# Making one of VectorE's four shifted exp copies with an accumulating DMA instead of a GpSimd copy

## The chip, the cores and the metric

The kernel runs on one core of one Trainium2 chip. The metric is the device time of one execution in microseconds (us), as the median of several runs.

## The reference

A transformer block with conditioning: 2048 tokens, width 512, 32 heads of 16, a feed-forward width of 1792. Cut to what matters:

```python
h = layernorm(x) * (1 + ca) + sa                       # ca, sa, ... from silu(c) @ w_mod
q, k, v = split(h @ wqkv)                              # 32 heads of 16
p = softmax(einsum('bhqd,bhkd->bhqk', q, k) / 4)       # 32 x 2048 x 2048 exps
x = x + ga * ((p @ v) @ wo)
h = layernorm(x) * (1 + cb) + sb
x = x + gb * ((gelu(h @ w_gate) * (h @ w_up)) @ w_down)
```

The 134 million exps are the load. In tiles of 128 x 512 they are 2048 "blocks".

## The kernel before

The program is unrolled by a planner in Python. It keeps a model of when each engine is free and when each DMA lands, and records the instructions of every engine in the order that this model suggests. On the chip each engine then runs its list strictly in order and waits on semaphores, so a wait that the planner did not foresee holds up everything behind it on that engine. TensorE writes the scores to tiles in PSUM, the memory for its results; the room for one block of scores is called a bank here. Where TensorE would stand idle the planner may put "filler" matmuls, whose result nobody reads.

ScalarE makes most exps, two or three blocks in one instruction. VectorE makes some "quads" (four blocks, one per head of a group) in another way: it turns the score into the bit pattern of a bfloat16 power of two, with one multiply and add to uint16, and makes four more copies with a constant added to the pattern. The sum of the five stands for the exponential better than one does, and TensorE adds them up in its accumulation of P times V. The copies are these tasks:

```python
SHIFT = (20, 43, 69, 101)          # constants added to the bit pattern

def shift_task(self, q, i):
    def f():
        s = self.sq_free[0]
        self.ts(self.helper, self.sq[s].bitcast(U16), self.kq[q["k"]].bitcast(U16),
                1.0, float(SHIFT[i]), ALU.mult, ALU.add)        # 128 x 2048, uint16
        # ... slot s becomes ready for the value matmuls
    self.task([f], ("shift", q["rnd"][0]), lambda: bool(self.sq_free) and self.first(q))
```

In the kernel before, `pooled` gives a copy to GpSimd (`self.helper = "pool"`) when GpSimd is free and its 1900 ns would not collide with a VectorE instruction for a port that, in the model, the two engines share (`port_at`):

```python
            if self.port_at(max(x, self.free["pool"]), 1900, "pool") <= t + 100:
                f()
```

The model lets a DMA land a fixed time after the bytes of all earlier DMAs.

```python
        if op.stream not in COMPUTE:
            self.free[eng] = t + 460
            self.dma_free = max(t + 1400, self.dma_free) + cost / 350
            op.t1 = self.dma_free + LAND                       # LAND = 1500 ns
```

How the softmax denominators come back: when a unit (512 queries of 4 heads) ends, its row sums go to DRAM, come back spread over 128 partitions, are inverted on VectorE, go to DRAM again and come back broadcast over the partitions; then VectorE multiplies. These are four dependent DMA steps, all issued on SyncE's queue, and at their end VectorE, in order, waits for the last:

```python
        self.dma("sp", s1..., self.osb[DH:P:32, lo:hi], ...)      # scr_den <- osb
        # den <- scr_den;  rden = 1 / den (VectorE);  scr_rec <- rden
        # rb <- scr_rec, four DMAs of up to 64 KB, broadcast to 32 partitions each
        def fin2():
            self.tt("dve", self.onorm[:, qd, c:c + W], osb, rb, ALU.mult)
```

The softmax here doesn't subtract the row's maximum and nothing guards it: scores larger than these inputs give would overflow.

Of the kernel before, what the change touches and what calls it, by code (L numbers as in the profile page):

```python
# [6 lines left out]
ALU = mybir.AluOpType  # L7
BF16 = mybir.dt.bfloat16
# [5 lines left out]
P = 128  # L14
# [28 lines left out]
AHEAD = 24  # L43
PREFER = 300
LAND = 1500
WIDE = 0
PRESS = 6
HOT = 1
FLOOR = 3300
POOLED = 1  # L50
FIRST = 30
AHEAD1 = 12
LATE = 0
# [39 lines left out]
class _Recorder:  # L93


    def __init__(self, nc):
        self.nc = nc
        self.ops = []
        self.count = {}
        self.bystream = {}  # L100
        self.clock = {e: {} for e in ALLENG}
        self.hist = {}
        self.pitch = {}
        self.kind = {}
        self.sem = {}
        self.dry = False
        self.probing = None
        self.free = {e: 700.0 for e in ALLENG}
        self.dma_free = self.pe_issue = self.pe_end = 0.0
        self.pe_mode = None  # L110
        self.tile_free = [0.0] * 16
        self.log = []
        self.whole = False
        self.lock = False
        self.port = []
        self.locked = 0
        self.fetched = [0, 0.0]

# [155 lines left out]

    def model(self, op, t, cost):
        eng = op.eng
        if op.stream not in COMPUTE:
            self.free[eng] = t + 460
            self.dma_free = max(t + 1400, self.dma_free) + cost / 350
            op.t1 = self.dma_free + LAND  # L280
        elif eng == "pe":
            cols, rows, tp = cost
            mode = 0 if tp is None else (1 if rows == 32 else 2)
            t = max(t, self.pe_issue)
            if self.fetched[0] % 128 == 0 and t > 20000:
                t = self.fetched[1] = max(t, self.fetched[1] + 3750)
            self.fetched[0] += 1
            if mode != self.pe_mode:
                t = max(t, self.pe_end + 105)
            q = range(16)  # L290
            if mode == 1:
                q = range(tp[0] // 8, tp[0] // 8 + 4)
            elif mode == 2:
                q = range(tp[1] // 32, 16, 4)
            t = max(t, max(self.tile_free[i] for i in q))
            end = t + max(cols, 64) / 2.4
            for i in q:
                self.tile_free[i] = end
            self.pe_mode, self.pe_issue, self.pe_end = mode, t + (4 if mode else 27), max(self.pe_end, end)
            self.free[eng] = t  # L300
            self.log.append((t, cols if mode == 0 else cols / 4))
            op.t1 = end + 158
        else:
            self.free[eng] = t + cost
            op.t1 = t + cost + (107 if eng == "act" else 92)
# [104 lines left out]
    def dma(self, eng, out, in_, sem, noncontig=False):  # L410
# [7 lines left out]
            n *= int(k)  # L418
        return self.rec(eng, fn, [in_], [out], dma=sem, cost=n)

    def emit(self, final):
        for s in self.count:
            self.sem[s] = self.nc.alloc_semaphore(s)
# [33 lines left out]
class _Kernel(_Recorder):  # L457
# [12 lines left out]
    def alloc(self):  # L470
# [16 lines left out]
                     for b in range(2)] for x in range(2)]  # L487
        self.sq = [mreg[:, 4096 + 2048 * i:6144 + 2048 * i] for i in range(NS)]
        self.sq += [mreg[:, 2048 * i:2048 * i + 2048] for i in range(2)]
        self.wmod = [mreg[:, 0:NDC * 1024].rearrange("p (a n) -> p a n", a=NDC),  # L490
                     mreg[:, NDC * 1024:NDC * 3072].rearrange("p (a n) -> p a n", a=NDC)]
        dreg = sb("dreg", [P, NFC * D], BF16)
# [27 lines left out]
        self.tcol = sb("tcol", [P, NDC], FP32)  # L520
        self.asum = self.rden[:, 0:2, 0:6]
        self.sc_bf = sb("sc_bf", [P, NDC], BF16)
        self.scbc = sb("scbc", [P, NDC, P], BF16)[:, :, :]
        self.modA = sb("modA", [P, 8], FP32)
        self.modB = sb("modB", [P, 8], FP32)
        self.rm4 = self.den[:, 0, 0:4]
        self.rm = sb("rm", [P, 2], FP32)
        self.ident = sb("ident", [P, P], BF16)
        self.ones = sb("ones", [P, P], BF16)[:, :]
        self.self32 = sb("self32", [P, P], FP32)  # L530
        self.scp = ps("ps_sc", [P, SC, 512], FP32)
        self.pv = ps("ps_pv", [P, 512], FP32)
        self.mi = ps("ps_mi", [P, 512], FP32)
        self.scr1 = self.dram("scr_den", [4, 2048], FP32)
        self.scr2 = self.dram("scr_rec", [4, 2048], FP32)


    def prologue(self):
# [29 lines left out]
        self.ts(dve, self.rm[:, 0:1], self.rm[:, 1:2], -1.0, 1.0, ALU.mult, ALU.add)  # L568
        self.memset(pool, self.vaug[:, :, :].rearrange("p t (h c) -> p t h c", c=VW)[:, :, :, DH:VW], 1.0)

        for dc in range(NDC):
            self.mm(self.scp[:, 0, dc:dc + 1], self.crow[0:1, P * dc:P * dc + P], self.ones[0:1, 0:1])
        self.warm_up(16)
# [238 lines left out]
    def side_mod(self):  # L812
        mi = self.mi[:, :]
        if not self.dry:
            self.task([lambda dc=dc: self.ts("dve", self.scbc[:, dc, :], self.ones, self.sc_bf[:, dc:dc + 1],
                                             None, ALU.mult) for dc in range(NDC)], "scbc")
        yield from self.until("scbc")
        for dst, k, s in ((self.ga, 2, 1.0), (self.gb, 5, 0.5)):
            for dc in range(NDC):
                yield 512, lambda dc=dc, k=k: self.mm(mi, self.scbc[:, dc, :], self.mod_w(dc, 512 * k, 512),  # L820
                                                      start=(dc == 0), stop=(dc == NDC - 1))
            self.ts("dve", dst[:, :], mi, s, None, ALU.mult)
            yield END
        yield 512, lambda: self.mod_cols(mi[:, 0:8], 1536)
        self.copy("dve", self.modB[:, :], mi[:, 0:8])
        self.ts("dve", self.modB[:, 4:8], self.modB[:, 4:8], 1.0, None, ALU.add)
        self.done("modB")
        if not self.dry:
            self.sq_free.extend(range(NS))
        yield END  # L830

    def side_wo_load(self):
# [236 lines left out]
                n += next((i for i, s in enumerate(steps) if s[0] != "dve"), len(steps))  # L1069
        return n  # L1070

    def pooled(self, t):

        for tk in self.tasks:
            if tk[1] is None or tk[1][0] != "shift" or not tk[2]() or self.urgency(tk) == 0:
                continue
            f = tk[0][0][1]
            self.helper = "pool"
            x = self.probe(f)
            if self.port_at(max(x, self.free["pool"]), 1900, "pool") <= t + 100:  # L1080
                f()
                self.tasks.remove(tk)
                self.done(tk[1])
                self.helper = "dve"
                return
            self.helper = "dve"

    def background(self, t):
        if POOLED and self.free["pool"] < t and self.busy():
            self.pooled(t)  # L1090
        while self.step("sp", max(self.free["sp"], t) + 40):
            pass
        while self.free["dve"] <= t + 150 and self.step("dve", max(self.free["dve"], t) + 40):
            pass
# [79 lines left out]
    def stream(self):  # L1174
# [45 lines left out]
        wait = self.wait = []  # L1220
        self.quad_free = list(range(NK))
        self.sq_free = [NS, NS + 1]
        cand = [k for k, (u, r, g0) in enumerate(rounds) if u in units[:2] or QA <= r * (512 // u[3]) < QB]
        quad = None
        self.helper = "dve"
# [56 lines left out]
        def pv_do(x):  # L1282
# [10 lines left out]
            else:  # L1293
                q["ready"].remove((i, src))
                q["n"] -= 1
                if i and (q["slots"][i] < NS or "modB" not in self.have):
                    self.sq_free.append(q["slots"].pop(i))
                q["used"].discard(i)
                self.drop(q)
# [8 lines left out]
        while cg <= group[units[-1]]:  # L1308
# [16 lines left out]
            if tq is not None and tq <= t + 30:  # L1325
# [10 lines left out]
                if len(mem) == CH and pos >= FIRST and not self.pressed() and self.free["dve"] + 600 < max(self.free["act"], t + 480) + 880 + LATE:  # L1336
                    while quad is None and cand and rounds[cand[0]][2] < pos + (AHEAD1 if rounds[cand[0]][2] < nsplit else AHEAD):
                        cand.pop(0)
                    if quad is not None:
                        g = quad["rnd"][2]  # L1340
                    elif (cand and self.quad_free and (pos < ends[2] or self.credit < CREDIT) and rounds[cand[0]][2] < pos + 96 and self.backlog() < BACK
                          and all(k in self.have for k in self.keys(seq[rounds[cand[0]][2]]))):
                        rnd = rounds[cand.pop(0)]
                        quad = {"rnd": rnd, "j": list(range(4)), "k": self.quad_free.pop(0), "ready": [], "n": 5, "slots": {}, "used": set(range(5))}
# [2 lines left out]
                        g = rnd[2]  # L1347
                        vec.update(range(g, g + 4))
                        mem, after = take(CH)
                gb = s0 + CH - 1  # L1350
                if g is not None:
                    for n in (CH, CH - 1):
                        if n == CH and (s0 or not WIDE or pos < nsplit + 12
                                        or self.probe(lambda: self.mm(self.scp[:, SC - 1, 0:P], *filler)) > t + 30):
                            continue
                        mem, after = take(n)
                        js = [j for j in quad["j"] if j not in [seq[m][2] for m in mem]]
                        if js:
                            break
                    if n == CH:  # L1360
                        gb = SC - 1
                    j = (js or quad["j"])[0]
                    quad["j"].remove(j)
                    g += j
                items = [(m, s0 + i) for i, m in enumerate(mem)]
                if g is not None:
                    items.append((g, gb))
                self.require(sorted({k for m, _ in items for k in self.keys(seq[m])}))
# [8 lines left out]
                if g is not None:  # L1377
                    kq = self.kq[quad["k"]]
                    while (self.free["dve"] + 1260 <= self.free["act"] + SLIP
                           and self.step("dve", max(self.free["dve"], t) + 40)):  # L1380
                        pass
                    self.ts("dve", kq[:, 512 * j:512 * j + 512].bitcast(U16), self.scp[:, gb, :], 128 / OCT, SHIFT_C,
                            ALU.mult, ALU.add)
                    if not quad["j"]:
                        quad["ready"].append((0, [kq[:, 512 * x:512 * x + 512] for x in range(4)]))
# [48 lines left out]

    def qk(self, items):
        for kk in range(max(512 // it[0][0][3] for it in items)):
            for ((_, qd, q0, W), r, j), k in items:
                kpb = 512 // W
                if kk >= kpb:
                    continue  # L1440
                kt = r * kpb + kk
                dc, ee = qd // 2, qd % 2
                self.mm(self.scp[:, k, W * kk:W * kk + W],
                        self.km[ee][32 * j:32 * j + 32, dc, P * kt:P * kt + P],
                        self.qT[32 * j:32 * j + 32, dc, q0:q0 + W], tp=(32 * j, 0))

# [23 lines left out]
# [4 lines that stand above are left out]
            self.ts(self.helper, self.sq[s].bitcast(U16), self.kq[q["k"]].bitcast(U16), 1.0, float(SHIFT[i]), ALU.mult, ALU.add)  # L1474
            if self.probing is None:
# [3 lines left out]
                q["ready"].append((i + 1, [self.sq[s][:, 512 * x:512 * x + 512] for x in range(4)]))  # L1479
                self.drop(q)  # L1480
        self.task([f], ("shift", q["rnd"][0]), lambda: bool(self.sq_free) and self.first(q))

    def osb_span(self, u):

# [202 lines left out]
```

## Time and profile before

| | before |
|---|---|
| median of 3 runs | 843.27 us (843.14 to 844.77) |
| profiled span | 842.2 us |
| ScalarE busy | 810.1 us, 96% |
| TensorE busy | 780.4 us, 93% |
| VectorE busy | 710.2 us, 84% |
| shifted copies on VectorE, on GpSimd | 284, 60 |
| exp blocks on ScalarE, on VectorE | 1704, 344 (86 quads) |

The groups of the kernel before, shapes kept apart: count, busy time and mean ns of one, then the engine's idle time just before them.

```profile
L364 ACT ACTIVATE E<-ps_sc 128x1536 bf16<-128x1536 f32 x320 | 453.7, 1538 | 3.1 <-PE ps_sc L351 2.8
L364 ACT ACTIVATE E<-ps_sc 128x1024 bf16<-128x1024 f32 x372 | 366.0, 1133 | 1.5 <-PE ps_sc L351 1.4
...
L376 POOL TENSOR_SCALAR mreg<-dreg 128x2048 uint16<-128x2048 uint16 x43 | 81.5, 1898 | 309.3 <-DVE mreg L376 92.3 <-PE ps_sc L351 75.8 <-DVE wreg L376 67.1
```

Busy time over count, 453.7 / 320 = 1.418 us for three blocks and 366.0 / 372 = 0.984 us for two, is what the prediction below takes as the cost of one exp, so 0.434 us a block. Both are a little high. Neighbouring exps overlap, and where their shapes differ the overlap is counted in both groups: the two sum to 819.7 us, more than ScalarE's 810.1 us in all. From the end of one exp to the end of the next, where ScalarE did not idle between, the trace has medians of 1.343 and 0.917 us, so 0.426 us a block. The exps waited 4.6 us in all.

```profile
rb<-scr_rec SPq DMA_DIRECT2D x96, 64.0 KB, 2.0
...
scr_rec<-rden SPq DMA_DIRECT2D x24, 8.0 KB, 1.4
```

### The profile page before, as it was taken

What the parts mean: (1) busy time and instruction counts of PE and PEld (TensorE: products, weight loads), DVE (VectorE), ACT (ScalarE), POOL (GpSimd) and SP (SyncE); (2) the same over time, 40 slices, a digit from 0 to 9 for tenths busy, and PEclk for the clock granted to TensorE, in tenths of its full rate; (3) what the DMA queues carried; (4) which work ended last, traced back from release to release, by engine and by line L of the source; (5) the groups of instructions that cost most, each with busy time, mean ns of one, the idle gap of its engine ahead of it and who ended that gap; (6) DMA issues with size and microseconds to landing.
All of it is one profiled execution on the core that took longest, in us unless ns stands there. A gap on an engine that the chain in (4) does not pass through costs nothing.

```text
span 842.2 us, 28224 instructions
## 1 busy us (share of the span) xinstructions
PE 780.4 (93%) x12684; PEld 278.9 (33%) x12689; DVE 710.2 (84%) x1345; ACT 810.1 (96%) x747; POOL 117.7 (14%) x71
## 2 busy tenths in 40 slices
PE   8899999999999998989999999899998998988997
PEld 3333333322222222222222222222343333335556
DVE  7878899899899999999889999999887886376484
ACT  5999999999999999999999999999999999999982
POOL 1000102031220331142210130333000000000000
PEclk9999999999999999999999999999999999999999
DMA  9000000000003111111003111111013222185330
GB/s 315 13 27 17 16 15 15 17 15 15 15 16 90 44 36 52 52 41 46 16 28 96 52 53 32 48 40 40 27 25 103 78 72 65 37 235 158 92 96 14
DMA packets 74931, 47.68 MB, mean 57 GB/s; under 512 B 17693, under 2 KB 70618, under 8 KB 74810
## 3 DMA queue, kind: packets, MB, share of 16 engines
q1 hardware_dynamic: 72426, 44.30, 18.1%
q8 instruction: 99, 1.62, 0.8%
q10 hardware_dynamic: 2384, 1.57, 0.7%
q14 instruction: 22, 0.18, 0.1%
HBM read 43.25 MB, written 2.61 MB: 54 GB/s over the span
## 4 chain that ended last, share of the span: by engine, by line
ACT 79%; PE 12%; DVE 4%; DMA 3%; SPq 1%; issue 0%; DVEq 0%
ACT E L364 76%; PE ps_mi L351 5%; PE ps_sc L351 5%; ACT wreg L364 3%; PE ps_pv L351 2%; DMA rb<-scr_rec 1%; DMA scr_rec<-rden 1%; SPq L415 1%; DVE mreg L376 1%; DVE wreg L381 0%; DMA xs<-in_A_x_dram 0%; DMA mreg<-in_B_w_down_dram 0%; DVE st L404 0%; DVE wreg L368 0%; DVE dreg L376 0%
## 5 line engine op out<-in xcount | busy, mean ns | idle before, releaser
L364 ACT ACTIVATE E<-ps_sc 128x1024 bf16<-128x1024 f32 (+2 forms) x700 | 782.7, 1311 | 17.4 <-PE ps_sc L351 16.9
L351 PE MATMUL ps_sc<-qT,kmo 32*128 32x512 bf16 (+2 forms) x1408 | 171.9, 323 | 10.5 <-ACT E L364 9.3
L351 PE MATMUL ps_sc<-qT,kme 32*128 32x512 bf16 (+2 forms) x1344 | 162.1, 331 | 18.2 <-ACT E L364 16.5
L376 DVE TENSOR_SCALAR dreg<-ps_sc 128x512 uint16<-128x512 f32 x228 | 153.9, 685 | 21.3 <-PE ps_sc L351 19.6
L351 PE MATMUL ps_pv<-E,vaug 128*17 128x512 bf16 (+2 forms) x2308 | 157.1, 321 | 1.3 <-DVE vaug L385 0.8
L351 PE MATMUL ps_pv<-mreg,vaug 128*17 128x512 bf16 (+2 forms) x1644 | 129.1, 354 | 4.1 <-DVE mreg L376 3.1
L376 POOL TENSOR_SCALAR mreg<-dreg 128x2048 uint16<-128x2048 uint16 x43 | 81.5, 1898 | 309.3 <-DVE mreg L376 92.3
L351 PE MATMUL ps_mi<-wreg,mreg 128*32 128x512 bf16 (+1 forms) x1792 | 113.7, 355 | 10.2 <-DVE wreg L381 5.5
L376 DVE TENSOR_SCALAR mreg<-dreg 128x2048 uint16<-128x2048 uint16 x185 | 119.6, 683 | 3.1 <-PE ps_pv L351 2.8
L351 PEld LDWEIGHTS ps_sc<-qT,kme 32*128 32x128 bf16 x1344 | 42.8, 91 | 146.5 <-ACT E L364 123.0
L376 DVE TENSOR_SCALAR mreg<-ps_sc 128x512 uint16<-128x512 f32 x116 | 78.5, 685 | 14.9 <-PE ps_sc L351 13.8
L351 PEld LDWEIGHTS ps_sc<-qT,kmo 32*128 32x128 bf16 x1408 | 46.4, 91 | 128.0 <-ACT E L364 101.7
L351 PEld LDWEIGHTS ps_pv<-E,vaug 128*17 128x17 bf16 x2308 | 47.6, 89 | 62.9 <-issue 50.8
L376 DVE TENSOR_SCALAR mreg<-mreg 128x2048 uint16<-128x2048 uint16 x99 | 65.1, 686 | 3.0 <-PE ps_pv L351 2.5
L351 PEld LDWEIGHTS ps_mi<-wreg,mreg 128*32 128x32 bf16 x1792 | 39.4, 95 | 57.4 <-issue 18.9
L351 PEld LDWEIGHTS ps_pv<-mreg,vaug 128*17 128x17 bf16 x1644 | 37.5, 88 | 51.0 <-DVE mreg L376 24.5
L385 DVE CAST wreg<-ps_mi 128x512 bf16<-128x512 f32 x49 | 33.6, 687 | 15.9 <-PE ps_mi L351 15.6
L376 POOL TENSOR_SCALAR mreg<-mreg 128x2048 uint16<-128x2048 uint16 x17 | 32.3, 1897 | 93.8 <-DVE onorm L368 23.0
L381 DVE SCALAR_TENSOR_TENSOR wreg<-wreg,ps_mi 128x512 bf16<-128x512 bf16 x49 | 33.4, 682 | 12.8 <-PE ps_mi L351 5.6
L351 PE MATMUL ps_mi<-hreg,wreg 128*32 128x512 bf16 x480 | 39.5, 384 | 0.5 <-DVE qT L376 0.5
L351 PE MATMUL ps_mi<-wo,onorm 128*32 128x512 bf16 x480 | 36.6, 382 | 0.1
L368 DVE TENSOR_TENSOR wreg<-wreg 128x1024 bf16<-128x1024 bf16 (+1 forms) x56 | 34.1, 618 | 0.5
(138 smaller groups left out, 597.8 us busy)
## 6 DMA issues: line engine op xcount, KB each, us to landing
mreg<-in_B_w_up_dram SPq DMA_DIRECT2D x32, 256.0 KB, 3.1
mreg<-in_B_w_gate_dram SPq DMA_DIRECT2D x28, 256.0 KB, 2.9
rb<-scr_rec SPq DMA_DIRECT2D x96, 64.0 KB, 2.0
mreg<-in_B_w_down_dram SPq DMA_DIRECT2D x16, 256.0 KB, 2.8
dreg<-in_B_w_down_dram SPq DMA_DIRECT2D x12, 256.0 KB, 4.0
mreg<-in_w_mod_dram SPq DMA_DIRECT2D x1, 2048.0 KB, 14.4
out_dram<-xs SPq DMA_DIRECT2D x16, 128.0 KB, 1.8
rb<-scr_rec SPq DMA_DIRECT2D x52, 32.0 KB, 2.6
```

What stands on the lines that cost most here:

```text
L351: return self.rec("pe", lambda e: e.matmul(out, lhsT, rhs, start=start, stop=stop, tile_position=tp), [lhsT, rhs], [out], cost=(n, int(rhs ...
L364: return self.rec("act", lambda e: e.activation(out, in_, func, scale=scale, **kw), rd, wr, cost=self.cost("act", out, [in_], "act"))
L368: return self.rec(eng, lambda e: e.tensor_tensor(out, a, b, op), [a, b], [out], cost=self.cost(eng, out, [a, b], "tt"))
L376: return self.rec(eng, lambda e: e.tensor_scalar(out, a, s1, s2, **kw), rd, [out], cost=self.cost(eng, out, [a], "ts"))
L381: return self.rec("dve", lambda e: e.scalar_tensor_tensor(out, a, s, b, op0=op0, op1=op1), rd, [out], cost=self.cost("dve", out, [a, b], " ...
L385: return self.rec(eng, lambda e: e.tensor_copy(out, in_), [in_], [out], cost=self.cost(eng, out, [in_], "ts"))
L415: return e.dma_start(out, in_)
```

## The change

Its intent: free GpSimd, and with it the port that the model keeps apart. One copy of a quad is made by a DMA that *adds* the bit patterns to a slot that already holds the constant. A plain DMA on SyncE's queue presets the slot (512 KB, one row of DRAM broadcast to 128 partitions); an accumulating DMA on GpSimd's queue adds the quad. There are two such slots. A second, smaller part lets a VectorE block go to a spare PSUM bank, so that ScalarE keeps three blocks in that instruction. Cut to its core:

```diff
-POOLED = 1
+ADDS = (3, 2)            # which of the four constants, one slot each
+ADDGEN = 1200
+ADDTIME = 5000
+SIDE = 1024
@@ model
+        if op.stream not in COMPUTE and eng == "pool":
+            self.free[eng] = t + ADDGEN
+            self.add_free = op.t1 = max(t + 2000, self.add_free) + ADDTIME
@@
+    def dma_add(self, out, in_, sem):
+        return self.rec("pool", lambda e: e.dma_start(out, in_, accum_op=ALU.add), [in_, out], [out], dma=sem)
@@
+    def preset(self, a):
+        self.task([("sp", lambda: self.dma("sp", self.aq[a].bitcast(U16),
+                    self.steps[a:a + 1, :].broadcast_to([P, 2048]), "dp%d" % a))], ("preset", a))
+
+    def added(self, t):
+        for q in self.wait:
+            if self.plain[q["rnd"][0]] <= ADDLEFT or q["adds"] >= ADDMAX:
+                continue
+            for a in range(len(ADDS)):
+                i = ADDS[a]
+                if ("preset", a) not in self.have or q["tk"][i] not in self.tasks:
+                    continue
+                # ... takes the shift task away and lets the DMA do it
+                op = self.dma_add(self.aq[a].bitcast(U16), self.kq[q["k"]].bitcast(U16), "dk%d" % a)
+                return
@@ background
-        if POOLED and self.free["pool"] < t and self.busy():
-            self.pooled(t)
+        if self.free["pool"] < t:
+            self.added(t)
@@ the spare bank for VectorE's block
-                        if n == CH and (s0 or not WIDE or pos < nsplit + 12 ...):
+                        if n == CH and (self.open or self.credit > SIDE
+                                        or self.probe(lambda: self.mm(self.mi[:, 0:P], *filler)) > t + 30):
```

(The rest makes room for a 4 KB slot per partition and writes the constants to DRAM once.)

More of the change, by code (lines that the diff above doesn't have):

```diff
@@ L45 @@
 LAND = 1500
-WIDE = 0
+SIDE = 1024
 PRESS = 6
@@ L49 @@
 FLOOR = 3300
-POOLED = 1
+ADDS = (3, 2)
+ADDGEN = 1200
+ADDTIME = 5000
+ADDLEFT = 7
+ADDMAX = 1
 FIRST = 30
@@ L115, in __init__ @@
         self.port = []
+        self.add_free = 0.0
         self.locked = 0
@@ L276, in model @@
         eng = op.eng
-        if op.stream not in COMPUTE:
+        if op.stream not in COMPUTE and eng == "pool":
+            self.free[eng] = t + ADDGEN
+            self.add_free = op.t1 = max(t + 2000, self.add_free) + ADDTIME
+        elif op.stream not in COMPUTE:
             self.free[eng] = t + 460
@@ L489, in alloc @@
         self.sq += [mreg[:, 2048 * i:2048 * i + 2048] for i in range(2)]
+        self.aq = [sb("aq", [P, 2048], BF16)[:, :], self.sq[NS - 1]]
         self.wmod = [mreg[:, 0:NDC * 1024].rearrange("p (a n) -> p a n", a=NDC),
@@ L522, in alloc @@
         self.sc_bf = sb("sc_bf", [P, NDC], BF16)
-        self.scbc = sb("scbc", [P, NDC, P], BF16)[:, :, :]
+        self.scbc = dreg[:, 11 * D:12 * D].rearrange("p (a n) -> p a n", a=NDC)
         self.modA = sb("modA", [P, 8], FP32)
@@ L528, in alloc @@
         self.ident = sb("ident", [P, P], BF16)
-        self.ones = sb("ones", [P, P], BF16)[:, :]
+        self.ones = dreg[:, 10 * D:10 * D + P]
         self.self32 = sb("self32", [P, P], FP32)
@@ L535, in alloc @@
         self.scr2 = self.dram("scr_rec", [4, 2048], FP32)
+        self.steps = self.dram("scr_add", [len(ADDS), 2048], U16)
     def prologue(self):
@@ L569, in prologue @@
         self.memset(pool, self.vaug[:, :, :].rearrange("p t (h c) -> p t h c", c=VW)[:, :, :, DH:VW], 1.0)
+        for i, x in enumerate(ADDS):
+            self.memset(dve, self.rb[0:16, 64 * i:64 * i + 64].bitcast(U16), SHIFT[x])
+        for i in range(len(ADDS)):
+            self.dma(sp, self.steps[i:i + 1, :].rearrange("o (p n) -> (o p) n", p=16),
+                     self.rb[0:16, 64 * i:64 * i + 64].bitcast(U16), "add%d" % i)
         for dc in range(NDC):
@@ L828, in side_mod @@
         if not self.dry:
-            self.sq_free.extend(range(NS))
+            self.sq_free.extend(range(NS - 1))
+            if len(ADDS) > 1:
+                self.preset(1)
+            else:
+                self.sq_free.append(NS - 1)
         yield END
@@ L1070, in backlog @@
         return n
-    def pooled(self, t):
-        for tk in self.tasks:
-            if tk[1] is None or tk[1][0] != "shift" or not tk[2]() or self.urgency(tk) == 0:
-                continue
-            f = tk[0][0][1]
-            self.helper = "pool"
-            x = self.probe(f)
-            if self.port_at(max(x, self.free["pool"]), 1900, "pool") <= t + 100:
-                f()
-                self.tasks.remove(tk)
-                self.done(tk[1])
-                self.helper = "dve"
+    def preset(self, a):
+        self.task([("sp", lambda: self.dma("sp", self.aq[a].bitcast(U16), self.steps[a:a + 1, :].broadcast_to([P, 2048]), "dp%d" % a))],
+                  ("preset", a))
+    def added(self, t):
+        for q in self.wait:
+            if self.plain[q["rnd"][0]] <= ADDLEFT or q["adds"] >= ADDMAX:
+                continue
+            for a in range(len(ADDS)):
+                i = ADDS[a]
+                if ("preset", a) not in self.have or q["tk"][i] not in self.tasks:
+                    continue
+                self.have.discard(("preset", a))
+                self.tasks.remove(q["tk"][i])
+                op = self.dma_add(self.aq[a].bitcast(U16), self.kq[q["k"]].bitcast(U16), "dk%d" % a)
+                self.kq_at[q["k"]] = op.t1
+                q["slots"][i + 1] = -1 - a
+                q["adds"] += 1
+                q["done"] = q.get("done", 0) + 1
+                q["ready"].append((i + 1, [self.aq[a][:, 512 * x:512 * x + 512] for x in range(4)]))
+                self.drop(q)
                 return
-            self.helper = "dve"
     def background(self, t):
-        if POOLED and self.free["pool"] < t and self.busy():
-            self.pooled(t)
+        if self.free["pool"] < t:
+            self.added(t)
         while self.step("sp", max(self.free["sp"], t) + 40):
@@ L1222, in stream @@
         self.sq_free = [NS, NS + 1]
+        self.kq_at = [0.0] * NK
+        self.preset(0)
         cand = [k for k, (u, r, g0) in enumerate(rounds) if u in units[:2] or QA <= r * (512 // u[3]) < QB]
@@ L1295, in pv_do @@
                 q["n"] -= 1
-                if i and (q["slots"][i] < NS or "modB" not in self.have):
+                if i and q["slots"][i] < 0:
+                    self.preset(-1 - q["slots"].pop(i))
+                elif i and (q["slots"][i] < NS or "modB" not in self.have):
                     self.sq_free.append(q["slots"].pop(i))
@@ L1340, in stream @@
                         g = quad["rnd"][2]
-                    elif (cand and self.quad_free and (pos < ends[2] or self.credit < CREDIT) and rounds[cand[0]][2] < pos + 96 and self.backlog() < BACK
+                    elif (cand and self.quad_free and self.kq_at[self.quad_free[0]] <= t + 300 and (pos < ends[2] or self.credit < CREDIT) and rounds[cand[0]][2] < pos + 96 and self.backlog() < BACK
                           and all(k in self.have for k in self.keys(seq[rounds[cand[0]][2]]))):
@@ L1349, in stream @@
                         mem, after = take(CH)
-                gb = s0 + CH - 1
+                gb = self.scp[:, s0 + CH - 1, :]
                 if g is not None:
                     for n in (CH, CH - 1):
-                        if n == CH and (s0 or not WIDE or pos < nsplit + 12
-                                        or self.probe(lambda: self.mm(self.scp[:, SC - 1, 0:P], *filler)) > t + 30):
+                        if n == CH and (self.open or self.credit > SIDE
+                                        or self.probe(lambda: self.mm(self.mi[:, 0:P], *filler)) > t + 30):
                             continue
@@ L1360, in stream @@
                     if n == CH:
-                        gb = SC - 1
+                        gb = self.mi[:, :]
                     j = (js or quad["j"])[0]
@@ L1364, in stream @@
                     g += j
-                items = [(m, s0 + i) for i, m in enumerate(mem)]
+                items = [(m, self.scp[:, s0 + i, :]) for i, m in enumerate(mem)]
                 if g is not None:
@@ L1381, in stream @@
                         pass
-                    self.ts("dve", kq[:, 512 * j:512 * j + 512].bitcast(U16), self.scp[:, gb, :], 128 / OCT, SHIFT_C,
+                    self.ts("dve", kq[:, 512 * j:512 * j + 512].bitcast(U16), gb, 128 / OCT, SHIFT_C,
                             ALU.mult, ALU.add)
@@ L1436, in qk @@
         for kk in range(max(512 // it[0][0][3] for it in items)):
-            for ((_, qd, q0, W), r, j), k in items:
+            for ((_, qd, q0, W), r, j), bank in items:
                 kpb = 512 // W
@@ L1442, in qk @@
                 dc, ee = qd // 2, qd % 2
-                self.mm(self.scp[:, k, W * kk:W * kk + W],
+                self.mm(bank[:, W * kk:W * kk + W],
                         self.km[ee][32 * j:32 * j + 32, dc, P * kt:P * kt + P],
@@ L1481, in shift_task @@
         self.task([f], ("shift", q["rnd"][0]), lambda: bool(self.sq_free) and self.first(q))
+        q.setdefault("tk", []).append(self.tasks[-1])
+        q["adds"] = 0
     def osb_span(self, u):
```

## The prediction

> **What bounds the kernel now.** ScalarE. The profile's busy table gives it 810.1 of 842.2 us (96%), and the chain of waits is 79% ScalarE. In the table of stretches it is busy 84.0 of 84.0 us in nearly every stretch from 168 to 672 us; what it lacks (about 32 us) lies before 20 us and after 790 us. The groups by form name the work: 320 exps of three score blocks (453.7 us busy, so 1.418 us each) and 372 of two (366.0, 0.984 each): one more 128x512 block costs ScalarE 0.434 us. They idled only 4.6 us. VectorE takes 344 of the 2048 blocks (86 quads) and also writes four shifted copies per quad: 284 of 344 itself, 60 on GpSimd (1.9 us each, 113.8 us).
>
> **What the change does.** The order of instructions, without times, says that 60 accumulating DMAs replace the same 60 GpSimd copies, with 62 presets of 512 KB on SyncE's queue. The gain is indirect: GpSimd's copies share a port with VectorE's fast copies, and the scheduler keeps the two apart; freed of this, and with a spare PSUM bank for ten blocks, it places 91 quads, not 86. ScalarE keeps 306 exps of three and 383 of two.
>
> - ScalarE: -14 x 1.418 + 11 x 0.984 = **-9.0 us**, nearly all on the critical path.
> - VectorE: +20 conversions and +20 copies of about 0.65 us = +26 us, to about 736 us (88%). It is over 90% busy between 168 and 588 us already: +1 us of waits.
> - TensorE: 76 fewer filler matmuls (428 to 352), 80 more value matmuls; even.
> - DMA: 62 presets and 60 adds of 512 KB, over 60 MB beside today's 47.7 MB: room at 20% use.
>
> **The risk is latency.** A program-order count, using the ScalarE times above, puts 7.9 to 15.5 us (median 11) of ScalarE work between an add's issue and its first consumer; about 1.5 us of that goes to the last conversion. The Trainium skill ("DMA: Bandwidth & Descriptors", Anatomy of one DMA) gives 2.0 us plus bytes/436e3; for 512 KB, 3.2 us for a plain copy. An add also reads its destination: I estimate 4 to 7 us. "SBUF — State Buffer" (SBUF: two separate sides) says VectorE's two-port operations starve GpSimd's descriptor writing; about 300 such copies remain, so I add 1 to 2 us. Most adds should then land in time and perhaps a tenth hold up TensorE by about 1 us, partly hidden: +1.5 us.
>
> **Prediction: 835.5 us**, 8 in 10 between 829 and 845. Chances: faster by over 2% 0.06, within 2% 0.88, slower by over 2% 0.06.
>
> **What would show each step.** Right: ScalarE busy near 801 us, with the same idle per exp group as before (under 10 us in all); GpSimd busy under 10 us of compute; VectorE busy 730 to 740 us; TensorE's waits on the added slot together under 5 us; issue to landing of adds 5 to 9 us; DMA volume near 110 MB. Wrong: ScalarE busy falls by 9 us but its idle before exps, released by TensorE, grows by as much, with TensorE waiting for the DMA of the added slot: then adds take over 10 us. Or VectorE's copies lengthen beyond 0.7 us: descriptor writing blocks the port. Or presets hold up the denominators' round trips on SyncE's queue.
>
> **What would make it wrong.** An add of 10 us or more would stall up to 60 times, in order, through TensorE: 850 to 880 us. A large gain needs more than the 20 blocks moved: the port conflict would have had to cost ScalarE time today, and its idle of 4.6 us says it does not.

## More of the kernel before

From the page of the kernel before: the busy times; the mean busy share of the DMA engines in 40 equal slices (a digit is tenths); the DMA queue of the program with its packets, MB and share of the 16 engines' span; and the chain of work that ended last, by engine.

```profile
PE 780.4 (93%) x12684; PEld 278.9 (33%) x12689; DVE 710.2 (84%) x1345; ACT 810.1 (96%) x747; POOL 117.7 (14%) x71
...
DMA  9000000000003111111003111111013222185330
...
q1 hardware_dynamic: 72426, 44.30, 18.1%
...
ACT 79%; PE 12%; DVE 4%; DMA 3%; SPq 1%; issue 0%; DVEq 0%
```

The chain is 79% ScalarE and only 3% DMA. After the loads at the start the DMA engines are nearly idle until late in the kernel.

The kernel before from 20 to 588 us, the stretch in which its GpSimd copies lie; `ACT busy` and `DMA share` are the columns to watch.

```profile
core 0: us, PE busy (x) PEld busy (x) DVE busy (x) ACT busy (x) POOL busy (x), PEclk, DMA share, GB/s
20.00:588.00 568.00, 533.33 (x7520) 162.42 (x7518) 522.24 (x929) 566.33 (x532) 114.27 (x61) 1.00 0.13 36
```

ScalarE idles 568 - 566.33 = 1.7 us here, with the DMA engines at 13%. I call this stretch the middle.

Two lines of the waits of the kernel before (who waited for whom: us in total, times, longest), and two of its DMA issues (KB each, median us from issue to landing).

```profile
ACT E L364 <- PE ps_sc L351: 16.9, 13, 2.9
...
DVE onorm L368 <- DMA rb<-scr_rec: 3.6, 3, 2.4
```

## The result, and the profile after

The changed kernel takes **865.54 us** (863.44 to 870.65, 4 runs) against 843.2 us (4 runs in the same rounds): ratio 1.027, 95% interval 1.0222 to 1.0317. It is slower, and outside the predicted range.

The page of the changed kernel, the lines that answer to those above; queue 0 is new and carries the adds.

```profile
PE 788.7 (91%) x12753; PEld 279.8 (32%) x12757; DVE 731.8 (85%) x1387; ACT 805.9 (93%) x744; POOL 61.1 (7%) x71
...
DMA  9022453554648567765556966885313222175330
...
q1 hardware_dynamic: 81418, 76.82, 29.3%
q0 software_dynamic: 8640, 31.46, 19.9%
...
ACT 37%; PE 25%; DVE 16%; DMA 15%; SPq 4%; issue 1%; ACTq 0%; DVEq 0%
```

The chain fell from 79% to 37% ScalarE, and DMA rose from 3% to 15%. The bytes of the program rose from 47.68 to 111.68 MB. The 31.46 MB of adds took 19.9% of the DMA engines' span; the 32.5 MB that queue 1 gained took 252.8 - 152.4 = 100.4 us of it (29.3% of 862.8 less 18.1% of 842.2), so **an added byte occupied the DMA engines 1.8 times as long as a preset byte**: 171.7 / 31.46 = 5.5 us per MB against 100.4 / 32.5 = 3.1. (In the experiments below, where only one of the two moves its bytes, it is 5.3 against 2.8.) An add and a preset also differ in their source and in the queue that issues them, so the factor is not shown to be the addition's alone.

The exps of the changed kernel, shapes kept apart; and its middle.

```profile
L372 ACT ACTIVATE E<-ps_sc 128x1536 bf16<-128x1536 f32 x306 | 434.6, 1518 | 11.0 <-PE ps_sc L359 10.5
L372 ACT ACTIVATE E<-ps_sc 128x1024 bf16<-128x1024 f32 x383 | 376.3, 1088 | 14.7 <-PE ps_sc L359 14.0
```

```profile
core 0: us, PE busy (x) PEld busy (x) DVE busy (x) ACT busy (x) POOL busy (x), PEclk, DMA share, GB/s
20.00:588.00 568.00, 523.18 (x7346) 158.10 (x7338) 513.44 (x919) 547.20 (x510) 55.49 (x59) 0.98 0.58 142
```

The counts are as forecast, 306 and 383. But their idle time went from 4.6 to 25.7 us. In the middle ScalarE idles 568 - 547.20 = 20.8 us instead of 1.7, and the DMA engines are busy 58% of the time instead of 13%. That is 19 us of the 20.6 us by which the span grew; another 4 us are idle after 800 us (42.2 - 22.7 = 19.5 us before, 62.8 - 38.9 = 23.9 us after), and 4 us less work pays for a part.

Waits of the changed kernel, and its DMA issues.

```profile
ACT E L372 <- PE ps_sc L359: 39.9, 38, 5.3
...
DVE onorm L376 <- DMA rb<-scr_rec: 18.7, 16, 2.9
...
PE ps_mi L359 <- DMA mreg<-in_B_w_gate_dram: 3.1, 2, 2.7
...
PEld ps_pv L359 <- DMA aq<-mreg: 2.7, 2, 1.8
...
PEld ps_pv L359 <- DMA mreg<-dreg: 2.3, 2, 1.2
...
PEld ps_pv L359 <- DMA mreg<-mreg: 1.8, 2, 1.6
...
PEld ps_pv L359 <- DMA aq<-dreg: 0.5, 1, 0.5
```

```profile
aq<-scr_add SPq DMA_DIRECT2D x35, 512.0 KB, 4.2
mreg<-scr_add SPq DMA_DIRECT2D x27, 512.0 KB, 4.6
aq<-dreg POOLq DMA_DIRECT2D x20, 512.0 KB, 5.3
...
rb<-scr_rec SPq DMA_DIRECT2D x96, 64.0 KB, 3.0
...
scr_rec<-rden SPq DMA_DIRECT2D x24, 8.0 KB, 3.6
```

The adds themselves land in 5.3 us in the largest group (all 60: 5.4 in the median, 8.7 at most), at the low end of the predicted 5 to 9. What changed more is what else uses DMA in that stretch: the 8 KB store of the inverted denominators takes 3.6 us instead of 1.4, their return 3.0 instead of 2.0. VectorE waits 18.7 us for that return in 16 places, where it waited 3.6 us in 3. From first issue to last landing, worked out from the issues and landings in the trace, a round trip in the middle takes 17.1 us in the median, against 12.3 before.

One such place, from the timeline of the changed kernel (start, duration, instruction, and in brackets the idle before it and what ended that; lines between are left out):

```profile
165.34 1.12 SPq L423 DMA_DIRECT2D rb<-scr_rec  x1
...
166.51 0.81 SPq L423 DMA_DIRECT2D mreg<-scr_add  x1
...
169.60 0.69 DVE L376 TENSOR_TENSOR onorm<-osb,rb 128x512 bf16<-128x512 f32 x1 [2.54 <-DMA rb<-scr_rec]
170.21 1.28 DVE L384 TENSOR_SCALAR dreg<-ps_sc 128x512 uint16<-128x512 f32 x2
...
170.95 0.38 PE L359 MATMUL ps_sc<-qT,kme 32*128 32x512 bf16 x1 [2.06 <-DVE dreg L384]
...
172.02 1.02 ACT L372 ACTIVATE E<-ps_sc 128x1024 bf16<-128x1024 f32 x1 [1.86 <-PE ps_sc L359]
```

The return of the denominators (`rb`) was issued at 165.34, in its fourth part, and a preset just behind it. VectorE stands for 2.54 us at the multiply that needs it. Behind the multiply, in VectorE's list, is the conversion of a score block that nothing stops but the order; until it is done its PSUM bank is not free, so TensorE waits 2.06 us, and then ScalarE 1.86 us. This is the path from a DMA that has nothing to do with the change to the engine that bounds the kernel.

### The profile page after: what moved, and what is told of

Same layout as the page of the kernel before. It is cut to its first block, busy times and chain, and to the rows that moved or that the text cites. A ratio compares the mean times of both kernels' runs of the same rounds, so it can differ in the third digit from the quotient of the medians. Undisturbed runs are those within 1.5% of the kernel's fastest.

```text
span 862.8 us, 28496 instructions
## 1 busy us (share of the span) xinstructions
PE 788.7 (91%) x12753; PEld 279.8 (32%) x12757; DVE 731.8 (85%) x1387; ACT 805.9 (93%) x744; POOL 61.1 (7%) x71
## 2 busy tenths in 40 slices
DMA packets 92565, 111.68 MB, mean 129 GB/s; under 512 B 19709, under 2 KB 72634, under 8 KB 92442
## 3 DMA queue, kind: packets, MB, share of 16 engines
q1 hardware_dynamic: 81418, 76.82, 29.3%
q0 software_dynamic: 8640, 31.46, 19.9%
## 4 chain that ended last, share of the span: by engine, by line
ACT 37%; PE 25%; DVE 16%; DMA 15%; SPq 4%; issue 1%; ACTq 0%; DVEq 0%
ACT E L372 35%; PE ps_mi L359 10%; PE ps_sc L359 9%; PE ps_pv L359 6%; DMA rb<-scr_rec 6%; DMA scr_rec<-rden 5%; SPq L423 4%; DVE mreg L384 4%; DVE dreg L384 3%; ACT wreg L372 2%; DVE wreg L376 2%; DMA xs<-in_A_x_dram 1%; DVE wreg L389 1%; DVE onorm L376 1%; DMA aq<-mreg 1%
## 5 line engine op out<-in xcount | busy, mean ns | idle before, releaser
L359 PE MATMUL ps_sc<-qT,kmo 32*128 32x512 bf16 (+2 forms) x1404 | 171.7, 324 | 11.8 <-ACT E L372 9.1
L359 PE MATMUL ps_sc<-qT,kme 32*128 32x512 bf16 (+2 forms) x1337 | 170.0, 335 | 13.5 <-ACT E L372 9.5
L384 DVE TENSOR_SCALAR mreg<-dreg 128x2048 uint16<-128x2048 uint16 x201 | 132.1, 683 | 4.6 <-PE ps_pv L359 4.5
L359 PE MATMUL ps_pv<-mreg,vaug 128*17 128x512 bf16 (+2 forms) x1680 | 125.7, 346 | 10.1 <-DVE mreg L384 6.4
L359 PE MATMUL ps_mi<-wreg,mreg 128*32 128x512 bf16 (+1 forms) x1792 | 116.2, 359 | 13.3 <-DVE wreg L389 5.6
L384 DVE TENSOR_SCALAR mreg<-ps_sc 128x512 uint16<-128x512 f32 x123 | 82.8, 684 | 15.5 <-PE ps_sc L359 14.3
L359 PEld LDWEIGHTS ps_sc<-qT,kme 32*128 32x128 bf16 x1337 | 44.6, 91 | 142.2 <-ACT E L372 105.1
L384 DVE TENSOR_SCALAR mreg<-mreg 128x2048 uint16<-128x2048 uint16 x103 | 67.3, 679 | 2.0 <-PE ps_pv L359 1.7
L376 DVE TENSOR_TENSOR onorm<-osb,rb 128x512 bf16<-128x512 f32 (+2 forms) x43 | 23.5, 548 | 18.7 <-DMA rb<-scr_rec 18.7
L359 PE MATMUL ps_mi<-mreg,hreg 128*32 128x512 bf16 x448 | 37.9, 384 | 0.0
```

What stands on the lines that cost most here:

```text
L359: return self.rec("pe", lambda e: e.matmul(out, lhsT, rhs, start=start, stop=stop, tile_position=tp), [lhsT, rhs], [out], cost=(n, int(rhs ...
L376: return self.rec(eng, lambda e: e.tensor_tensor(out, a, b, op), [a, b], [out], cost=self.cost(eng, out, [a, b], "tt"))
L384: return self.rec(eng, lambda e: e.tensor_scalar(out, a, s1, s2, **kw), rd, [out], cost=self.cost(eng, out, [a], "ts"))
```

## The experiments

Theory A: the added bytes crowd the DMA engines; other transfers land late; VectorE and TensorE wait in order. Rivals: B, the presets' own waits hold up SyncE's in-order queue; C, the adds land too late for their readers; D, VectorE's fast copies and GpSimd's descriptor writing block each other; and the spare bank itself.

Where I say "same order", the list of every engine was compared with that of the changed kernel and differs only in the operands named (the runs with small presets also have one more memset on GpSimd at the start).

### Small presets, small adds, both small (same order)

```diff
 # e1: the preset moves 16 of its 2048 columns; waits and plan are for the whole
-self.dma("sp", aq[a], steps[a:a + 1, :].broadcast_to([P, 2048]), ...)
+self.dma("sp", ..., moved=(aq[a][:, 0:16], steps[a:a + 1, 0:16].broadcast_to([P, 16])))
 # e2: the same for the add
-e.dma_start(out, in_, accum_op=ALU.add)
+e.dma_start(out[:, 0:16], in_[:, 0:16], accum_op=ALU.add)
 # e3: both
```

In e1 the adds work on bfloat16 rather than on uint16, because a slot that is never reset would run over. These results are wrong; the comparison with the reference passed all the same, since one of five copies of a minority of blocks weighs little against its tolerance.

> The changed kernel with the same order of instructions on every engine, but each of the 62 presets moves 16 columns instead of 2048 (4 KB instead of 512 KB); issue, waits and the plan are unchanged; the adds work on bf16 so that the slot stays finite. Wrong result on purpose. Theory A (bytes: presets and adds crowd the DMA engines, so that the short transfers of the denominators and the weight loads land late and VectorE and TensorE, which run in order, wait for them): about half of the loss goes, 845 to 855 us, and VectorE's wait for the returned denominators falls from 18.7 us to under 10 us. Theory B (the presets' waits on SyncE's in-order queue hold up the transfers behind them): stays at 862 to 868 us, since every wait is still there. Theory C (the adds themselves land too late): stays above 860 us.

> The changed kernel with the same order of instructions on every engine, but each of the 60 adds moves 16 columns instead of 2048; presets are whole. Wrong result on purpose. Theory A: about half of the loss goes, 845 to 855 us. Theory B: 862 to 868 us. Theory C: the adds land in 2 to 3 us instead of 5.3, and most of the loss goes, 835 to 845 us.

> Both the presets and the adds move 16 columns; same order, same waits, same number of descriptors' rows. Wrong result on purpose. Theory A: all of the loss goes and the gain that was predicted from the 20 blocks shows: 833 to 839 us, ScalarE idle before its exps 5 to 12 us, VectorE waits for the returned denominators under 5 us. Theory B: 855 us or more. A fourth theory D (VectorE's fast copies and GpSimd's descriptor writing block each other): stays above 850 us, since 128 rows a transfer still need descriptors.

| | median us | ratio to before (95%) | DMA share, middle | ScalarE idle, middle | VectorE's wait for the return | round trip, median |
|---|---|---|---|---|---|---|
| before | 844.41 | | 0.13 | 1.7 us | 3.6 us | 12.3 us |
| changed | 865.54 | 1.027 (1.0222 to 1.0317) | 0.58 | 20.8 | 18.7 | 17.1 |
| small presets | 846.41 | 1.0022 (0.9997 to 1.0046) | 0.43 | 6.3 | 12.0 | 15.5 |
| small adds | 839.35 | 0.9945 (0.993 to 0.996) | 0.33 | 1.6 | 2.8 | 14.4 |
| both small | 840.7 | 0.9968 (0.9932 to 1.0005) | 0.17 | 1.9 | 2.7 | 13.6 |

(The row "before" has the median of these rounds and the profile above; the changed kernel's ratio is to the runs of before in its own rounds.) The middle with small adds, columns as above:

```profile
20.00:588.00 568.00, 535.63 (x7654) 163.53 (x7648) 531.50 (x951) 566.37 (x531) 55.11 (x61) 1.00 0.33 94
```

B falls as a cause of its own: with small adds, and with both small, every preset still waits in SyncE's queue where it did, and the loss is gone. SyncE waited 53.3 us in 26 places for the value matmuls that set the slots free in the changed kernel, and more, 75.0 us in 32 places, with small adds. D falls: the descriptors for 128 rows are still written (queue 0 has 8640 packets in the changed kernel and in all three of these runs), and VectorE's copies take 683 ns in the changed kernel as they did before. Bytes are the cause.

My "half each" was wrong: taking away either half removes most of the loss, and taking away the adds' bytes removes all of it; by its time alone, that run fell in the range that I had given to theory C. With small presets the wait for the return fell to 12.0 us, not under 10; with both small the time was 840.7 us, above my 833 to 839. The plan has slack. At 33% busy DMA engines a round trip of 14.4 us still fits; at 43% and 15.5 us it begins not to, and at 58% ScalarE idles 21 us. And it matters whose bytes they are: the 8 KB store takes 3.3 us with the adds whole, 1.5 us with the presets whole, though both runs move about 80 MB.

C is not settled by small adds, as they also land sooner (2.5 us instead of 5.3). But with small presets the adds landed in 5.1 us, no wait of TensorE for an add is left in its list of waits, and most of the loss was gone, where C had forecast over 860 us. The runs below go further.

They also show what the change would gain if its DMAs were free: about 3 to 5 us (ratios 0.9968 and 0.9945), of the 9 that I counted. ScalarE's busy time does fall to 801.7 us as forecast, but with small adds it starts a microsecond later (9.55 us busy before 20 us, against 10.52) and idles 21.4 us after 800 us, against 19.5.

### The spare bank alone, and the adds alone

```diff
 # e4: the kernel before with the spare-bank part of the change only
 # e11: the changed kernel without that part
-SIDE = 1024
+SIDE = -10 ** 9
```

> The kernel before with one part of the change alone: the spare PSUM bank may take VectorE's block, and GpSimd's copies stay. The plan then keeps 344 blocks on VectorE, with 326 exps of three and 363 of two: ScalarE minus 3 us by the durations of the kernel before. If the bank is harmless, 838 to 844 us; if the bank's use by score blocks itself costs TensorE waits, over 846 us.

> The changed kernel planned without the spare bank for VectorE's blocks: the adds alone, 55 of them, 57 presets. The plan then keeps the 86 quads, 320 exps of three and 372 of two of the kernel before, so ScalarE's work is that of before. If traffic costs what it cost in the changed kernel: about 843 plus 15 to 20 us, 855 to 866 us. If the spare bank was what made the changed kernel slow: 840 to 850 us.

The bank alone: 846.69 us, ratio 1.0031 (1.0017 to 1.0046), ScalarE idle in the middle 2.0 us. It costs a little, and not in the middle; my other reading (838 to 844) missed. The adds alone: 872.78 us, ratio 1.0344 (1.0322 to 1.0366), above my range of 855 to 866, with the work of ScalarE as before, 19.3 us of idle in the middle and 24.5 us of VectorE's wait for the return. The spare bank is not what makes the change slow; without it the adds gain no quad at all.

### Taking away the waits, with all bytes moved (same order)

```diff
 # e5: VectorE's multiply reads a tile that it need not wait for
-self.tt("dve", onorm, osb, rb, ALU.mult)
+self.tt("dve", onorm, osb, osb, ALU.mult)       # planned at the same time
 # e9: the value matmuls of an added slot read a tile that landed long ago
-self.mm(acc, v, aq_slot_part, ...)
+self.mm(acc, v, self.filler[1], ...)            # planned at the same time
 # e10: both
```

Their outputs are wrong, which doesn't matter for the times. The reads were moved, and with them the waits went, so nothing races. With the reads of an added slot one more wait goes: its next preset no longer waits on SyncE for the value matmuls (0 such waits without the add wait and 0.4 us with neither, against 53.3 us in the changed kernel). What the second and third run gain can therefore not be split between TensorE's wait for the adds and SyncE's for the slots. The first run keeps SyncE's waits (48.0 us).

> The changed kernel in the same order on every engine, all bytes moved, but VectorE's normalisation reads the unnormalised outputs twice instead of the denominators that come back from DRAM, so that it no longer waits for that transfer. Wrong result on purpose. If the late denominators are the main road by which the crowded DMA engines reach ScalarE (VectorE waited 18.7 us for them in the changed kernel, 3.6 us before): 845 to 855 us. If the late weights and late adds, for which TensorE itself waits, are the main road: 858 us or more.

> The changed kernel in the same order, all bytes moved, but the value matmuls of the added slots read a tile that has long been there instead of the slot, so that TensorE never waits for an add. Wrong result on purpose. In the changed kernel TensorE's waits for adds come to about 7 us (weight loads, 7 times), and the run without the denominators' wait kept 8.2 us of ScalarE idle between 20 and 588 us. If late adds are a second, smaller road: 856 to 862 us, ScalarE busy 550 to 555 us of 568 in that stretch against 547.2. If late adds were the main road after all: under 850 us.

> Both waits taken away at once, in the same order and with all bytes moved. Wrong result on purpose. If these two roads are nearly all by which the crowded DMA engines reach ScalarE: 838 to 844 us, ScalarE busy 563 us or more of 568 between 20 and 588 us. If late weight loads or the engines' own slowing under traffic matter as well: 845 us or more, ScalarE under 562 us.

| | median us | ratio to before (95%) | ScalarE idle, middle | DMA share, middle |
|---|---|---|---|---|
| changed | 865.54 | 1.027 (1.0222 to 1.0317) | 20.8 us | 0.58 |
| no wait for the returned denominators | 848.14 | 1.0061 (1.0017 to 1.0105) | 8.2 | 0.60 |
| no wait for the adds | 856.75 | 1.0144 (1.011 to 1.0177) | 13.8 | 0.59 |
| neither | 843.3 | 0.9986 (0.9958 to 1.0014) | 6.5 | 0.60 |

The middle without the wait for the denominators, and then without both waits, columns as above:

```profile
20.00:588.00 568.00, 528.94 (x7541) 161.55 (x7539) 525.91 (x941) 559.77 (x523) 55.27 (x61) 1.00 0.60 146
```

```profile
20.00:588.00 568.00, 533.79 (x7576) 162.31 (x7573) 526.75 (x945) 561.53 (x526) 56.02 (x61) 0.99 0.60 147
```

The traffic is the same, and nearly all of the loss goes with the waits. So busy DMA engines hardly slow the compute engines themselves (a score matmul of 512 columns takes 384 ns with neither wait, as before); they act through waits. The denominators' return is the larger (about 17 us by the medians, 18 by the ratios), that for the added slots the smaller (9 or 11), together 22 or 24 since they overlap in part. C is at most a part of the truth, not the main part. I had expected 563 us or more of ScalarE in the middle with neither wait, and got 561.5. The waits that are left suggest a third road, which no run takes away: late weight loads (TensorE waited for those of the gate in 3 places, 3.8 us) and the earlier steps of the round trip (4.3 us at the inversion).

### Planning for later landings, and fewer adds

```diff
 # e6: the plan allows 1.5 us more for each step of the denominators' trip
-            op.t1 = self.dma_free + LAND
+            op.t1 = self.dma_free + LAND + (1500 if op.stream[:4] in ("d_da", "d_db", "d_dc", "d_dd") else 0)
 # e7: one slot
-ADDS = (3, 2)
+ADDS = (3,)
 # e12: one slot, and an add only while no denominators are under way
+ADDS = (3,)
-        if self.free["pool"] < t:
+        if self.free["pool"] < t and not self.live:
             self.added(t)
 # e8: no adds, and no copies on GpSimd either
-        if self.free["pool"] < t:
-            self.added(t)
```

> The changed kernel planned anew, with 1.5 us more allowed for each of the denominators' transfers, so that VectorE's in-order queue reaches their users later; 63 adds and 65 presets, 89 VectorE quads instead of 91. If a stale allowance for landings is what turns traffic into waits, a good part returns: 845 to 856 us, with VectorE's wait for the returned denominators under 10 us. If the plan's allowance does not matter: 860 us or more.

> The changed kernel planned with one accumulating slot instead of two: 36 adds and 37 presets, so about 40% fewer added bytes, and 89 VectorE quads. From the two small-transfer runs, removing half of the added bytes removed nearly all the loss: 840 to 848 us if bytes decide. If the loss came from the adds' latency or their in-order waits one by one, it scales with their number: about 854 us.

> The changed kernel planned with no adds at all: VectorE makes every shifted copy, GpSimd makes none, and the plan still reaches 85 quads, against 86 before with 60 copies on GpSimd and 91 with 60 adds. It shows what the offload is worth. ScalarE carries 4 more blocks than before: 840 to 848 us, no DMA waits beyond those of the kernel before.

> A kernel with a right result, planned so that an add is issued only while no unit's denominators are under way, with one slot: 16 adds, 17 presets, 88 VectorE quads (314 exps of three, 377 of two: ScalarE minus 3.6 us by the durations of the kernel before). If the denominators' round trips are the main road and few bytes do no harm: VectorE's wait for the returned denominators under 5 us, ScalarE busy 565 us or more of 568 between 20 and 588 us, 839 to 845 us; it would beat the kernel before only if the plan's end after 800 us does not lengthen. If each add costs its share of the loss however it is placed: ScalarE 561 us or less in that stretch.

Planning later (63 adds) did what it should to VectorE and nothing for the time: 866.02 us, ratio 1.0236 (1.018 to 1.0291). Its waits:

```profile
PE ps_mi L359 <- DMA mreg<-in_B_w_gate_dram: 7.6, 3, 5.3
...
PEld ps_pv L359 <- DMA aq<-dreg: 6.3, 4, 2.3
...
DVE onorm L376 <- DMA rb<-scr_rec: 5.6, 4, 2.8
...
PEld ps_pv L359 <- DMA aq<-mreg: 4.1, 4, 1.8
```

VectorE's wait for the return fell to 5.6 us, but the waits for late weights and late adds rose in its place (7.6 us for the gate's weights in 3 places, up to 5.3 at once), and ScalarE idles 18.1 us in the middle. The wait is where my first reading had it (under 10 us), the time where my second had it (860 or more): allowing for one kind of transfer is not enough where others are late too.

One slot (36 adds): 858.31 us, ratio 1.0164 (1.014 to 1.0187), missing both of my ranges. In the middle the loss does shrink to 6.9 us of idle at 41% DMA share, as the small-transfer runs say; but this plan ends badly, with one wait of 11.9 us for TensorE that ends near 835 us. Its total can't decide between bytes and number; its middle agrees with bytes. No offload at all: 851.11 us, ratio 1.0076 (1.0049 to 1.0102), above my 840 to 848, with 1.8 us of idle in the middle, the loss lying in the later part of the plan.

Adds between trips (16 adds) gave a right result and 847.05 us, ratio 1.0014 (0.9992 to 1.0037), above my 839 to 845. VectorE's wait for the return is 0.8 us. ScalarE idles 5.3 us in the middle at 26% DMA share, between my two forecasts; what is left are the gate's weights (TensorE's weight loads waited 3.6 us in 2 places) and the inversion (3.8 us). It is the best kernel with adds, and it does not beat the kernel before. No run with a right result did.

## Why the prediction was wrong

- **ScalarE bounds the kernel; 20 blocks fewer are worth 9 us of its work.** Right about the work: 801.7 us busy with small adds, against a forecast of 801. Of it about 5 us reach the time with the small adds, which move little, and 3 with both small; start and end take the rest.
- **"DMA: 62 presets and 60 adds of 512 KB, over 60 MB beside today's 47.7 MB: room at 20% use."** This is the step that failed. The volume was right (111.68 MB). The share was not: an add held the engines nearly twice as long per byte as a preset, and the mean over the kernel hid that everything was added to one stretch, which went from 13% to 58%. And "room" is no answer for a kernel whose lists wait in order for small transfers: they became late long before the engines were full, a cost for which the prediction has no term. From the table, in this plan 33% cost nothing, 43% about 5 us of idle, 58% about 19. That is no threshold: adds between trips, in another plan, had 5.3 us of idle at 26%.
- **The adds' latency.** I predicted 4 to 7 us and 1 to 2 for starved descriptors; they took 5.3 us, mostly in time. "An add of 10 us or more" as the way to fail was wrong: the loss came with adds of 5.3 us. The stall term of 1.5 us for late adds was too small: TensorE's weight loads waited 7.3 us for adds, and taking those waits and the presets' away gave 9 us.
- **The sign that I named last, "presets hold up the denominators' round trips on SyncE's queue", was the right symptom** and I gave it no number. Its mechanism was not the queue: with presets that wait as before and move little, or with whole presets and small adds, the trips are harmless.
- **VectorE.** Predicted 730 to 740 us busy, measured 731.8; its copies kept their 683 ns. The port conflict was not the trouble.

What stays open is the clock's share. TensorE's mean granted clock was 0.988 in the changed kernel, 1.0 before and 0.998 with small adds. In the middle of the changed kernel the trace has it at 0.5 in three spells, 17 us in all (from 238.4, 276.0 and 463.7 us), where a score matmul takes 602 ns instead of 385; there are none in the middle before, with small adds, with both small, or without the wait for the denominators at the same traffic. Two of the three begin within 0.2 us of the end of TensorE's longest stalls (2.7 us for a weight, 3.0 us behind VectorE's wait for the return). ScalarE idled 7.2 of its 20.8 us in these spells, so up to a third of the loss in the middle may be the clock's, on top of the waits; that stalls bring the spells about is suggested by their times, and not tested. With neither wait, one more such spell, where TensorE waited 1.9 us for the gate's weights, holds 3.5 of the 6.5 us of idle that are left. The ends of the plans after 588 us differ by several us from plan to plan, and no run isolates why.

## What to carry to other kernels

Before moving work from an idle engine to DMA, list every other transfer of that stretch that something waits for in order, and ask what those will take with the new traffic beside them; cost the DMA engines' time in that stretch, not over the kernel, and measure an accumulating transfer (here it held them nearly twice as long as a plain one of its size). To see which wait carries the loss, let the reader take other data at the same place in the same order: if the time comes back with all bytes still moving, it was the wait, and the bytes only made it long. Check which other waits went with the read.

## What the Trainium skill lacked or had wrong

- "DMA: Bandwidth & Descriptors", Issuing engines are not separate DMA queues, says that DMAs of all engines run on the same 16 engines and interleave. The runs agree; what it lacks is a figure for what this costs another queue's transfers. Here adds on GpSimd's queue, with small presets, lengthened the round trips on SyncE's queue from 13.6 us (both small) to 15.5.
- The same page, Anatomy of one DMA, has no cost for an accumulating DMA. Here 512 KB landed in 5.1 us with small presets beside it and 5.3 us with whole ones, where its formula gives 3.2 us for a copy; and it held the DMA engines 5.5 us per MB against 3.1 for a plain broadcast.
- The same page, Latency and other measured facts, gives HBM latency as 0.2 us on average and 2 us at high load. It does not say at what load dependent small transfers suffer. Here an 8 KB store went from a median of 1.4 us to 3.6 us, at 13% and 58% busy DMA engines in the middle; and the share alone does not tell, as it took 1.5 us at 33% (presets) and 3.3 us at 43% (adds).
- "SBUF — State Buffer", SBUF: two separate sides, warns that VectorE's two-port operations starve a DMA that GpSimd issues. Beside a VectorE that was 90% busy in the middle, the instruction that issues an add took 0.85 us in the median and at most 1.37 us, and 16-column adds landed in 2.5 us: no starvation that mattered here. Which of VectorE's instructions used two ports the trace does not tell.
